# Forming the phases and exponents of lag factors with TensorE instead of VectorE and ScalarE, in an S4 convolution and SwiGLU kernel

## The chip, the cores and the metric

The kernel runs on one core of a Trainium2 chip. The core has five engines, each with a queue of its own that is worked off in order: TensorE (PE, matmuls and transposes; its weight loads are shown as PEld), VectorE (DVE), ScalarE (ACT), GpSimd (POOL) and SyncE (SP, which issues most DMAs). Matmul results land in PSUM, everything else lies in SBUF or in DRAM. The metric is the time of one execution in microseconds on the device; less is better.

## The reference

Two layers of two blocks each, on a sequence of L = 2048 rows of D = 512 channels. The first block is a state space convolution (N = 128 states for each channel), the second a SwiGLU feed-forward net. Cut to what matters:

```python
dt = exp(log_dt)[:, None]                       # one for each channel
logdA = dt * (A_re + 1j * A_im)                 # [D, N]
dB = dt * (B_re + 1j * B_im)
P = exp(logdA[:, :, None] * arange(L))          # [D, N, L]
K = einsum("dn,dnl,dn->dl", Cc, P, dB).real     # the filter, one for each channel
y = irfft(rfft(pad(u)) * rfft(pad(K)))[:L] + u * Dskip

x = x + A_ref(layernorm(x))                     # convolution with K
x = x + (silu(n @ w_gate) * (n @ w_up)) @ w_down    # n = layernorm(x)
# both twice, with the same weights and the same K
```

The change touches only the way in which the factors of P are made. A power l of the exponential is split as l = 32 a + b. For each channel d and state n the kernel needs the phase th = dt * A_im / (2 pi) and the rate rho = dt * A_re. The *lag factors* are, for a = 1 to 64, exp(32 a rho) times cosine and sine of the turns 32 a th; the *small powers* are exp(b (rho + 2 pi i th)) for b = 1, 2, 4, 8, 16, out of which all b below 32 are multiplied together. TensorE then sums over n the product of the two, which gives K at all lags.

## The kernel before

The states n lie on the 128 partitions. The filters are made in stage 1, a loop over eight chunks of DC = 64 channels; behind it come the convolutions by DFT and the feed-forward blocks for eight blocks of 512 rows. In stage 1 the order of ACT, DVE and PE is written out by hand (a `manual_schedule`): generators (`gen_turns`, `gen_reduce`, `gen_trig`, `gen_exp`, `gen_g`, `gen_e`) issue one step each time that `take` asks for it, and each engine works its steps off in the order of issue. POOL and SP run their own issues in order as well. The loop body of iteration i does several things side by side: the lag sums of chunk i, the products of chunk i+1, the phases, sines and exponents of chunk i+2. The first two chunks are made in a head in front of the loop, and the lag sums of the last chunk behind it.

For one chunk, by function and line of the kernel before:

- `gen_turns`: DVE forms the turns 32 a th for a = 17 to 32 in `t16` (L349, 1024 elements for each partition), and the turns of the five small powers in `xi` (L352, 320 elements). The factors stand in `am`, a table of 21 columns.
- `gen_reduce`: ACT rounds to whole turns by writing an integer (L360 for the small powers, L366 for six pieces of `re`, since a = 1 to 16 are halves, quarters and so on of the upper ones); DVE subtracts (L369, and L372 six times). What is left is below half a turn.
- `gen_trig`: ACT takes Abs (L379), sine (L380) and cosine (L381), in three trios: the small powers, the upper half of a, the lower half.
- `gen_exp`: ACT takes exponentials of rho with 32 a as its scale, five for the small powers (`mz`, L389), 20 for `re` (a to 32) and 19 for `mu` (a = 33 to 63) at L394, and fills the other a by squares (L397).
- `gen_e`: DVE multiplies exponentials into cosines and sines (L407, L410, L413, L416).
- `gen_g`: DVE multiplies `mz` into the small powers (L424), starts with the weights w0 (L427 to L431), and doubles the powers in the levels 1, 2, 4, 8, 16 (L437, L441, L445, L446).
- `lags` (L456, L457): PE sums over the states, 128 matmuls into `pk`, in a large PSUM buffer. `spread_in` (ACT, `ks`, L462), `spread` (PE, `kp`, L472) and a copy on ACT (`kt`, L949) bring the filter into the form that the spectra need.
- `spectra`: PE multiplies by the DFT matrix (`pw`, L493, eight matmuls for each of four spectra), ACT copies out (`s1`, L502), POOL combines (L504), SP stores.

Between these steps stand pieces of other work: `second` and `direct` (spectra of the input blocks, `pf`, L276, copied out by ACT, L279), and `norms` (ACT squares, L306, and PE sums `nrm`, L310, for the scale factors of the weights). There are two large PSUM buffers (`pbig`: pk, kp and others) and four small ones (`psml`: pw, pf, nrm and others), each handed out in turn, so that a matmul into a buffer waits for the engine that reads the one before it there.

In the head, `turns()` scales rho and th and takes exponents and turns between the statistics of the first x rows.

## Time and profile before

| what | value |
| --- | --- |
| median of 3 runs | 1213.28 us (1213.07 to 1215.39) |
| profiled execution, span from first to last instruction | 1210.1 us; no other time is shown for it |
| PE busy in the span | 1104.0 us (91%) |
| DVE | 1048.5 us (87%) |
| ACT | 646.3 us (53%) |
| POOL | 187.8 us (16%) |
| DMA moved | 138.66 MB |

The first row is what is compared. The others belong to one profiled execution, whose span is 3.2 us below the median. Busy shares are means over the whole span: the first quarter, the stage that the change touches, looks different from the rest. In the page's row of 40 slices (30 us each), DVE stands at 8 to 9 tenths and ACT at 7 to 9 in the first nine slices, PE at 7 to 9 behind the first; from the tenth slice on PE is at 8 to 9 tenths in all but the last few and ACT falls to 2 to 7.

In rows of the trace, "out<-in" are the program's names of the tiles, "128x1024 f32" is partitions by elements, xN the number of instructions in a group, then come busy time in us, and the mean of one in ns. A row of the timeline has start and length in us, engine, line, operation, and, in brackets, how long the engine had stood idle before and what released it. "clock" is the TensorE clock that the chip granted, as a share of the full one.

### The profile page before, as it was taken

The numbers are of one execution on the slowest core, as the hardware profiler recorded it, in microseconds if no ns is written. First come the engines' busy times: TensorE is split into PE (matmuls) and PEld (weight loads), VectorE is DVE, ScalarE is ACT, GpSimd is POOL, SyncE is SP. The second block draws the span as 40 slices with busy tenths as digits, with TensorE's granted clock in tenths as the row PEclk, the third lists the DMA queues.
The fourth block names the chain that finished last, engine by engine and source line by source line (L and its number), as shares of the span: only waits on it lengthen the run. The fifth ranks groups of instructions, "written<-read, shape, count | busy, mean of one in ns | idle before, by whom it ended". The sixth has DMA issues, their size and how long they took to land.

```text
span 1210.1 us, 25368 instructions
## 1 busy us (share of the span) xinstructions
PE 1104.0 (91%) x10220; PEld 858.5 (71%) x10220; DVE 1048.5 (87%) x1677; ACT 646.3 (53%) x1392; POOL 187.8 (16%) x209
## 2 busy tenths in 40 slices
PE   3877988888978998989999999999999999999998
PEld 2755766666976776868686777778686776867875
DVE  8999999999869999999998999999992799983221
ACT  7999999973265545526753524664431553324111
POOL 1116343453220010101100000121000010000000
PEclk9999998889999999999999999999999999999999
DMA  6223233236389427433245353424433144311000
GB/s 226 96 88 92 72 89 86 73 107 184 116 285 264 127 67 199 133 118 88 62 157 140 105 179 133 125 79 146 140 118 129 33 119 132 117 58 44 14 23 18
DMA packets 134857, 138.66 MB, mean 115 GB/s; under 512 B 75921, under 2 KB 85137, under 8 KB 134738
## 3 DMA queue, kind: packets, MB, share of 16 engines
q1 hardware_dynamic: 132178, 128.64, 35.4%
q0 software_dynamic: 2560, 8.39, 2.0%
q8 instruction: 80, 1.31, 0.5%
q14 instruction: 39, 0.32, 0.1%
HBM read 98.71 MB, written 28.31 MB: 105 GB/s over the span
## 4 chain that ended last, share of the span: by engine, by line
DVE 32%; PE 27%; issue 5%; DMA 4%; ACT 2%; POOL 2%; SPq 1%; DVEq 0%; ACTq 0%; POOLq 0%
DVE t L683 5%; PE pgu L807 5%; PE pgu L808 5%; PE pgu L809 5%; DVE yk L686 4%; DVE z L216 3%; DVE yk L683 3%; PE py L821 3%; PE py L822 3%; PE py L823 3%; PE pi L702 2%; DVE sg L813 2%; DVE hl L815 1%; DVE yl L216 1%; DVE bt L216 1%
## 5 line engine op out<-in xcount | busy, mean ns | idle before, releaser
L807 PE MATMUL pgu<-mix,wsl 128*128 128x256 f16 x1280 | 350.5, 274 | 7.9 <-DVE sg L813 4.4
L809 PE MATMUL pgu<-mix,wsl 128*128 128x256 f16 x1280 | 350.5, 274 | 1.2 <-DVE wsl L579 1.2
L808 PE MATMUL pgu<-mix,wsl 128*128 128x256 f16 x1280 | 350.4, 274 | 0.0
L808 PEld LDWEIGHTS <-wsl 128*128 128x128 f16 x1280 | 125.8, 98 | 24.6 <-issue 8.6
L821 PE MATMUL py<-wsl,hh 128*128 128x512 f16 (+1 forms) x352 | 134.6, 382 | 9.3 <-DVE xg L826 5.3
L809 PEld LDWEIGHTS <-wsl 128*128 128x128 f16 x1280 | 125.8, 98 | 16.5 <-DVE wsl L579 1.5
L807 PEld LDWEIGHTS <-wsl 128*128 128x128 f16 x1280 | 125.8, 98 | 15.8
L823 PE MATMUL py<-wsl,hl 128*128 128x512 f16 (+1 forms) x352 | 134.4, 382 | 2.4 <-DVE hl L815 2.4
L812 ACT ACTIVATE sg<-pgu,sc 128x512 f32<-128x512 f32 x80 | 54.5, 682 | 128.8 <-PE pgu L809 110.9
L822 PE MATMUL py<-wsl,hh 128*128 128x512 f16 x320 | 122.1, 382 | 0.0
L683 DVE TENSOR_TENSOR t<-uu,w 128x1024 f32<-128x1024 f32 x96 | 116.8, 1217 | 5.5 <-DMA uu<-udr 5.3
L686 DVE TENSOR_TENSOR yk<-yk,t 128x1024 f32<-128x1024 f32 x96 | 116.7, 1215 | 0.1
L493 PE MATMUL pw<-kt,ek 128*128 128x256 f32 (+2 forms) x420 | 105.4, 392 | 0.0
L813 DVE SCALAR_TENSOR_TENSOR sg<-pgu,sc,sg 128x512 f32<-128x512 f32 x80 | 59.6, 744 | 52.3 <-ACT sg L812 52.0
L702 PE MATMUL pi<-yl,mix 128*128 128x256 f16 x672 | 91.4, 273 | 5.5 <-ACT yl L691 3.5
L493 PEld LDWEIGHTS pw<-kt,ek 128*128 128x128 f32 x420 | 83.9, 208 | 11.9
L814 ACT ACTIVATE hh<-sg 128x512 f16<-128x512 f32 x80 | 50.0, 626 | 67.6 <-DVE sg L813 67.6
L211 POOL TENSOR_TENSOR rs<-mv,mhalf 128x2 f32<-128x2 f32 (+1 forms) x21 | 38.7, 1845 | 275.7 <-ACT mv L210 275.6
L260 PE MATMUL pf<-z,eh 128*128 128x256 f16 x576 | 74.4, 272 | 1.6 <-ACT z L250 1.6
L702 PEld LDWEIGHTS <-mix 128*128 128x128 f16 x672 | 65.3, 98 | 14.3 <-issue 3.9
L691 ACT ACTIVATE yl<-mix,sy 128x512 f16<-128x512 f32 x56 | 40.2, 717 | 61.4 <-DVE mix L688 61.2
L504 POOL COPY w0r<-s 128x128 f32<-128x128 f32 x29 | 48.1, 1659 | 141.7 <-ACT s L502 122.2
(221 smaller groups left out, 2292.0 us busy)
## 6 DMA issues: line engine op xcount, KB each, us to landing
w<-wdr SPq DMA_DIRECT2D x96, 256.0 KB, 2.8
uu<-udr SPq DMA_DIRECT2D x96, 256.0 KB, 3.0
udr<-u POOLq DMA_DIRECT2D x32, 256.0 KB, 2.8
wdr<-wo SPq DMA_DIRECT2D x96, 64.0 KB, 2.0
udr<-u SPq DMA_DIRECT2D x16, 256.0 KB, 2.5
n<-ndr SPq DMA_DIRECT2D x16, 256.0 KB, 3.0
n<-xdr SPq DMA_DIRECT2D x4, 1024.0 KB, 6.0
xg<-in_A_u_dram SPq DMA_DIRECT2D x3, 1024.0 KB, 7.4
```

The costliest lines, as they stand in the source:

```text
L260: PE.matmul(pf[:, o], lhsT=e, rhs=m, start=k == 0, stop=k == len(terms) - 1)
L493: PE.matmul(pw[:, i], lhsT=e, rhs=kt[:, :, c + 4 * k0:4 * k1:4, :].rearrange("p g k d -> p k g d"), start=c == 0, stop=c == 3)
L683: V.tensor_tensor(t, uu.unsqueeze(1).to_broadcast([P, 2, 2, HD]), w.unsqueeze(2).to_broadcast([P, 2, 2, HD]), OP.mult)
L686: V.tensor_tensor(yk, yk, t, OP.add)
L702: PE.matmul(pi[:, o], lhsT=e, rhs=m, start=k == 0, stop=k == len(terms) - 1)
L807: PE.matmul(o, lhsT=wgu(wi, k, 0)[:, fs], rhs=nh[:, k], start=k == 0, stop=False)
L808: PE.matmul(o, lhsT=wgu(wi, k, 0)[:, fs], rhs=nlo[:, k], start=False, stop=False)
L809: PE.matmul(o, lhsT=wgu(wi, k, 1)[:, fs], rhs=nh[:, k], start=False, stop=k == 3)
L813: V.scalar_tensor_tensor(sg, pgu[:, 1], sc6[:, 4:5], sg, OP.mult, OP.mult)
L821: PE.matmul(py[:, r], lhsT=hh[:n, f, rc], rhs=wd(f, 0)[:n], start=f == 0, stop=False)
L822: PE.matmul(py[:, r], lhsT=hh[:n, f, rc], rhs=wd(f, 1)[:n], start=False, stop=False)
L823: PE.matmul(py[:, r], lhsT=hl[:n, f, rc], rhs=wd(f, 0)[:n], start=False, stop=f == FT - 1)
```

## The change

PE now multiplies rates by a table. The table `am` becomes 1712 columns wide: for 16 channels at a time, it has the factors 32 a for a = 1 to 63 (exponents, `TA`), 32 a for a = 1 to 32 (phases, `TM`) and 1, 2, 3, 4, 8, 16 (small powers, `TZ`), each in the row of its own channel and nought in those of the others, and this three times, once for each bf16 part of the rate. It is loaded as float32 (128 x 1712, 0.88 MB), fourth on SP's queue, ahead of x and B, into `amf`, and ACT converts it to bf16 in `tabs` (L893).

- `gen_parts` (new, for two chunks at a time): ACT takes the bf16 part of rho and th (L365), DVE the residue (L367), ACT its bf16 part (L369), DVE the rest (L371), and SP issues two DMA transposes (L373) that put rows of (rho or th, part, channel) on the partitions. It runs for chunks 0 and 1, and 2 and 3, in the head, and for the pairs behind them in the iterations 1 and 3.
- `args` (new, L377): one bf16 matmul with 112 rows for a group of 16 channels.
- `gen_turns`: four such matmuls of 512 columns into two large PSUM buffers `pp`, and four of 96 into a small one, `pz`.
- `gen_reduce`: ACT rounds from PSUM (L404, twice 1024 and once 384), DVE subtracts (L407, the same three).
- `gen_trig`: the same trios (L414 to L416), channels 0 to 31 first, then 32 to 63, small powers last.
- `gen_exp`: four matmuls of 96 and one exponential for `mz` (L425), then eight times one matmul into a small buffer `pm` (L377) and one exponential out of it (L435), four for `re`, four for `mu`. The squares are gone.
- `gen_g`: six small powers instead of five; the powers 1, 2, 3 are made in one step (L474, L475, L477, L478), then levels 4, 8, 16 as before.
- Loop and head ask for the steps in another order. In the body, two of the four `mu` exponents of chunk i+1 and the fourth spectrum of chunk i-1 stand between the lag sums and `ks`, and the last two operations of `gen_g` stand behind the last of `gen_e`.

The core of the diff:

```diff
+    am = np.zeros((2, 4, 16, NA), np.float64)
+    ta, tm, tz = am[..., :1008], am[..., 1008:1520], am[..., 1520:]
+    zs = (1, 2, 3, 4, 8, 16)
+    for d in range(16):
+        ta[0, :3, d, 63 * d:63 * d + 63] = 32.0 * np.arange(1, 64)
+        tm[1, :3, d, 32 * d:32 * d + 32] = 32.0 * np.arange(1, 33)
+        for x in range(2):
+            tz[x, :3, d, (16 * x + d) * NZ:(16 * x + d + 1) * NZ] = zs
...
+    def gen_parts(ch):
+        src = rt[:, :, ch * DC:(ch + 2) * DC].rearrange("p x (g d) -> p x g d", d=16)
+        hi, mid, lo = (pt[:, :, :, :, q].rearrange("p c g x d -> p x (c g) d") for q in range(3))
+        A.activation(hi, src, AF.Copy)
+        yield
+        V.tensor_tensor(r1, src, hi, OP.subtract)
+        yield
+        A.activation(mid, r1, AF.Copy)
+        yield
+        V.tensor_tensor(lo, r1, mid, OP.subtract)
+        for c in range(2):
+            nc.sync.dma_start_transpose(lts[(ch + c) % 3], pt[:, c].rearrange("p g x q d -> p (g x q d)"))
+        yield
+    def args(o, ch, g, tab):
+        PE.matmul(o, lhsT=lts[ch % 3][:112, g], rhs=tab, start=True, stop=True)
...
     def gen_turns
-        V.tensor_tensor(t16, am[:, 5:].unsqueeze(1).to_broadcast([P, DC, 16]),
-                        t_.unsqueeze(2).to_broadcast([P, DC, 16]), OP.mult)
-        V.tensor_tensor(xz[1], am[:, :5].unsqueeze(2).to_broadcast([P, 5, DC]), t_.unsqueeze(1).to_broadcast([P, 5, DC]), OP.mult)
+        for h in range(2):
+            pp = pbig([P, 32, 32], "pp")
+            for g in range(2):
+                args(pp[:, 16 * g:16 * g + 16], ch, 2 * h + g, TM)
...
     def gen_reduce
-            A.activation(k, src, AF.Copy, scale=1.0 / st)
-            V.scalar_tensor_tensor(*part, OP.mult, OP.subtract)
+        for p, k in zip(pz, ks):
+            A.activation(k, p, AF.Copy)
+        for p, k, o in zip(pz, ks, outs):
+            V.tensor_tensor(o, p, k, OP.subtract)
...
     def gen_exp
-                A.activation(o[:, :, a - a0], r_, AF.Exp, scale=32.0 * a)
+                pm = psml([P, 16, 32], "pm")[:, :, :n]
+                args(pm, ch, g, TA[:, :, a0:a0 + n])
+                A.activation(ts[2][:, 16 * g:16 * g + 16, 1:] if a0 else re[:, 16 * g:16 * g + 16, 1:33], pm, AF.Exp)
...
     def gen_g
-        for n in (1, 2, 4, 8, 16):
+        zr, zi = (t[:, :3].rearrange("p l d -> p d l").unsqueeze(1).to_broadcast([P, 2, DC, 3]) for t in xz)
+        new, tmp = g[:, :, :, 1:4], tmp8[:, :, :, :3]
+        V.tensor_tensor(new, g[:, :, :, 0:1].to_broadcast([P, 2, DC, 3]), zr, OP.mult)
+        V.tensor_tensor(tmp, g[:, ::-1, :, 0:1].to_broadcast([P, 2, DC, 3]), zi, OP.mult)
+        V.tensor_tensor(new[:, 0], new[:, 0], tmp[:, 0], OP.subtract)
+        V.tensor_tensor(new[:, 1], new[:, 1], tmp[:, 1], OP.add)
+        for lv, n in ((3, 4), (4, 8), (5, 16)):
...
     for i in range(NCH - 1):
-            take(ex, 100)
+            take(ex, 3)
             take(sp, 2)
+            take(ex, 3)
             norm_units(3, 9)
             norm_units(0, 0)
+            take(ex, 3)
```

How the order of the queues moves is shown at three places. First, PE behind the lag sums `pk` of a chunk in the middle of the loop. Before, the fourth spectrum `pw` and then the sums `nrm` follow at once:

```order
L457 MATMUL pk<-im,g 32x64
L493 MATMUL pw<-kt_489,ef 128x256
L493 MATMUL pw<-kt_489,ek_84 128x256 x3
L493 MATMUL pw<-kt_489,ef 128x256
L493 MATMUL pw<-kt_489,ek_84 128x256 x3
L310 LDWEIGHTS onesb
L310 MATMUL nrm<-sq,onesb 128x344
```

In the changed kernel PE at the same place has matmuls of rates (in the transposed parts `tt`) by the table (`tabs`) into `pm`, ahead of that spectrum and behind it:

```order
L503 MATMUL pk<-im,g 32x64
L377 LDWEIGHTS tt
L377 MATMUL pm<-tabs,tt 128x16x31
L539 MATMUL pw<-kt_465,ef 128x256
L539 MATMUL pw<-kt_465,ek_85 128x256 x3
L539 MATMUL pw<-kt_465,ef 128x256
L539 MATMUL pw<-kt_465,ek_85 128x256 x3
L377 LDWEIGHTS tt
L377 MATMUL pm<-tabs,tt 128x16x31
```

The spectrum and all behind it, `nrm` and the spreading `kp` among it, have moved behind exponent matmuls. Second, PE between the first and the second spectrum of the same iteration's own chunk. Before, one follows the other:

```order
L493 MATMUL pw<-kt_489,ef 128x256
L493 MATMUL pw<-kt_489,ek_83 128x256 x3
L493 MATMUL pw<-kt_489,ef 128x256
L493 MATMUL pw<-kt_489,ek_83 128x256 x3
L493 MATMUL pw<-kt_489,ef 128x256
L493 MATMUL pw<-kt_489,ek_84 128x256 x3
```

Now PE has two exponent matmuls between them (`wx` is another place of transposed parts):

```order
L539 MATMUL pw<-kt_465,ef 128x256
L539 MATMUL pw<-kt_465,ek_84 128x256 x3
L539 MATMUL pw<-kt_465,ef 128x256
L539 MATMUL pw<-kt_465,ek_84 128x256 x3
L377 LDWEIGHTS wx
L377 MATMUL pm<-tabs,wx 128x512
L377 LDWEIGHTS wx
L377 MATMUL pm<-tabs,wx 128x512
L539 MATMUL pw<-kt_465,ef 128x256
L539 MATMUL pw<-kt_465,ek_85 128x256 x3
```

The two matmuls use the small PSUM buffers that spectra and exponents share. Third, ACT behind the copy `ks` in an odd iteration. Before, ACT rounds the turns that lie in SBUF (`xi`, `t`), in seven pieces:

```order
L462 ACTIVATE ks<-pk 128x1024
L360 ACTIVATE xr<-xi 128x320
L366 ACTIVATE re<-t_996 128x64x16
L366 ACTIVATE re<-t_996 128x64x8
L366 ACTIVATE re<-t_996 128x64x4
L366 ACTIVATE re<-t_996 128x64x2
L366 ACTIVATE re<-t_996 128x64 x2
L502 ACTIVATE s_1093<-pw 128x512
L379 ACTIVATE xr<-xi 128x320
```

Now ACT rounds three pieces out of PSUM, and in iterations 1 and 3 the two steps of `gen_parts` (`btl<-rt` is L365's bf16 part) stand behind them:

```order
L508 ACTIVATE ks<-pk 128x1024
L404 ACTIVATE re<-pp 128x32x32 x2
L404 ACTIVATE xr<-pz 128x384
L365 ACTIVATE btl<-rt 128x2x8x16
L369 ACTIVATE btl<-btl 128x2x8x16
L548 ACTIVATE s_1032<-pw 128x512
L414 ACTIVATE re<-im 128x32x32
```

The rounding of the large pieces has moved ahead of that of the small powers, and the spectrum's copy stands behind the parts.

More of the change, by code (lines that the diff above doesn't have):

```diff
@@ L882 @@
         take(fw[3], 1)
+        for f in fw[4:6]:
+            next(f)
         for h in range(2):
@@ L936 @@
             take(sp, 1)
+            take(rd, 1)
             kp = spread(i, ks)
@@ L947 @@
                 take(tr, 1)
+            else:
+                tr = iter(())
             kt = kt2[:, i % 2]
```

240 lines of the change are left out of this document (130 added, 110 removed).

## The prediction

> **What bounds the kernel now.** I read the page's first line, the span, then the busy time by stretches, cut at two marks of VectorE's own timeline: 57.93 us, where it begins the products of chunk 1 (L424), and 288.17, where it begins the first L683 after the last chunk.
>
> ```profile
> span 1210.1 us, 25368 instructions
> ```
> ```profile
> 57.93:259.00 201.07, 167.72 (x2227) 129.14 (x2220) 200.53 (x275) 188.29 (x488) 85.12 (x77) 0.91 0.29 82
> 259.00:288.17 29.17, 24.87 (x441) 19.52 (x444) 28.89 (x38) 13.15 (x39) 15.91 (x13) 1.00 0.44 127
> ```
>
> The columns are length, busy PE, PE loads, DVE, ACT, POOL, granted clock, DMA share, GB/s. In the loop over chunks DVE works 200.53 of 201.07 us: it is the bound. ACT works 188.29 and PE 167.72 at a mean clock of 0.91, so both have less than a fifth to spare. The change touches only this first stage; all behind it starts when the last chunk is done, so what this stage gains or loses passes through whole.
>
> **What DVE sheds.** Groups of the first 300 us, eight chunks; the first four rows are by line, the others keep shapes apart.
>
> ```profile
> L349 DVE TENSOR_TENSOR t<-am,th 128x1024 f32<-128x1024 f32 x8 | 10.9, 1368 | 0.0
> L352 DVE TENSOR_TENSOR xi<-am,th 128x320 f32<-128x320 f32 x8 | 4.7, 585 | 0.0
> L369 DVE TENSOR_TENSOR xi<-xi,xr 128x320 f32<-128x320 f32 x8 | 4.4, 546 | 0.1
> L372 DVE SCALAR_TENSOR_TENSOR im<-t,re 128x64 f32<-128x64 f32 (+4 forms) x48 | 27.1, 597 | 0.0
> ```
> ```profile
> L372 DVE SCALAR_TENSOR_TENSOR im<-t,re 128x1024 f32<-128x1024 f32 x8 | 9.7, 1213 | 0.0
> L437 DVE TENSOR_TENSOR g<-g,xr 128x512 f32<-128x512 f32 x8 | 6.3, 783 | 0.0
> L437 DVE TENSOR_TENSOR g<-g,xr 128x256 f32<-128x256 f32 x8 | 3.3, 418 | 0.0
> L437 DVE TENSOR_TENSOR g<-g,xr 128x128 f32<-128x128 f32 x8 | 3.3, 408 | 0.0
> L445 DVE TENSOR_TENSOR g<-g,tmp 128x128 f32<-128x128 f32 x8 | 2.3, 284 | 0.0
> L445 DVE TENSOR_TENSOR g<-g,tmp 128x64 f32<-128x64 f32 x8 | 3.4, 425 | 0.0
> ```
>
> Phases: (10.9 + 4.7 + 4.4 + 27.1) / 8 = 5.9 us a chunk go. Levels 1 and 2 go, each shape twice (L441 and L446 repeat them): 2 x (0.408 + 0.418 + 0.284 + 0.425) = 3.1. In come two subtractions of 1024 from PSUM, 2 x 1.21 by the 1024 row, one of 384 at about 0.6, the joint step (two of 384, two of 192: 2 x 0.6 + 2 x 0.37, between the neighbouring rows), and half of two 256-element operations for the parts, 0.4: 5.4. So DVE sheds 3.6 a chunk, some 21 us over the six full iterations. If PSUM made the three subtractions half as dear again, 1.5 of that would go. This is the gain on offer, and it counts only as long as DVE waits for nobody.
>
> **Who waits now.** Steps that one engine did from its own inputs become chains: PE multiplies, ACT rounds or exponentiates, DVE subtracts, ACT takes sines. In each iteration the order has ACT and PE alternate, each behind the other in its queue. So I walk one iteration by rows. First ACT, then PE (times are starts; the difference of two starts is what the first costs):
>
> ```profile
> 169.11 0.47 ACT L379 ACTIVATE xr<-xi 128x320 f32<-128x320 f32 x1 [0.65 <-DVE xi L369]
> 169.60 1.28 ACT L380 ACT_TABLE_LOAD   x1
> 170.90 0.47 ACT L380 ACTIVATE xi<-xi 128x320 f32<-128x320 f32 x1
> ...
> 171.72 1.00 ACT L949 ACTIVATE kt<-kp 128x1024 f32<-128x1024 f32 x1
> 172.63 1.09 ACT L379 ACTIVATE re<-im 128x1024 f32<-128x1024 f32 x1
> ...
> 175.85 0.58 ACT L279 ACTIVATE u<-pf 128x512 f32<-128x512 f32 x1
> ...
> 184.44 1.23 ACT L306 ACTIVATE sq<-st 128x344 bf16<-128x344 f32 x3
> ...
> 186.16 0.58 ACT L502 ACTIVATE s<-pw 128x512 f32<-128x512 f32 x1
> 186.65 1.91 ACT L394 ACTIVATE re<-rho 128x64 f32<-128x64 f32 x12
> ```
> ```profile
> 191.93 0.34 PE L456 MATMUL pk<-re,g 128*32 128x64 f32 x8
> ...
> 197.34 0.70 PE L493 MATMUL pw<-kt,ef 128*128 128x256 f32 x2
> ...
> 200.90 0.60 PE L310 MATMUL nrm<-sq,onesb 128*128 128x344 bf16 x3
> 201.43 0.64 PE L472 MATMUL kp<-ks,ident 128*32 128x256 f32 x8
> ...
> 204.35 0.70 PE L276 MATMUL pf<-n,ef 128*128 128x256 f32 x2
> ...
> 207.91 0.59 PE L493 MATMUL pw<-kt,ef 128*128 128x256 f32 x2
> ```
> ```profile
> 64.94 1.42 PE L310 MATMUL nrm<-sq,onesb 128*128 128x512 bf16 x3 [2.03 <-ACT sq L306]
> ...
> 83.79 1.44 PE L310 MATMUL nrm<-sq,onesb 128*128 128x512 bf16 x3 [3.02 <-ACT sq L306]
> ...
> 88.45 0.61 PE L493 MATMUL pw<-kt,ef 128*128 128x256 f32 x2
> ```
> ```profile
> 99.30 0.81 PE L310 MATMUL nrm<-sq,onesb 128*128 128x512 bf16 x3
> ```
>
> ACT: table 1.3, the trio Abs, Sin, Sin of 1024 3.2, that of the small powers 1.3, a copy of 1024 0.9, of 512 out of PSUM 0.5, three squares 1.2. PE: pk 5.4, a spectrum pw 3.5, kp 2.9, pf 3.5, three nrm 0.5, a bf16 matmul of 512 columns 0.25 (0.81 for three).
>
> Rows have the lines of the kernel before; from here on, lines named without a row are those of the changed kernel. Time 0 is the start of pk. The matmul of the second mu exponent now stands behind pk: 5.7. The fourth spectrum follows to 9.2, and only behind it the third mu matmul, 9.4. ACT: that exponent to 9.9, squares 11.1, the last mu 11.6, ks 12.5, the first rounding of phases 13.4. DVE's order has L464 to L470 (some 2.3), four products of 1024 (4.8), the joint step (1.9) and level 4 (two of 512, two of 256: 2.4) ahead of L407, which needs this rounding: ready at 11.4, it waits for 13.4 and is through at 14.6. ACT meanwhile: second rounding 14.3, small one 14.8, s1 15.3, then table and first trio 19.8, kt 20.7, second trio 23.9, u 24.4, small trio 25.7, table 27.0, mz 27.5, first exponent 28.0. PE: kp waits for L407 (their big PSUM buffer), 14.6 to 17.5, pf 21.0, pz 21.3, first spectrum 24.8, pm 25.0. The next pm needs the small PSUM buffer that mz empties, 27.5, and the second spectrum the buffer of the first exponent: it starts at 28.0 instead of 25. To 31.5; nrm and pm 32.3; third spectrum 35.8; two pm, and the next pk starts at 36.3. DVE, from 14.6 on, has 17 us left and ends near 32: it is idle for 4 and no longer sets the pace. PE does 29.7 us of work and waits for the rest; the three bf16 us that it got are on the path.
>
> Iteration 0 has no fourth spectrum: 33.9. Iterations 1 and 3 also form parts: ACT's L365 stands behind the roundings, 15.2, DVE's L367 needs it and stands ahead of L407. Behind L367 come two operations of 512, one of 1024, two of 256 and the low part before L407 (0.42 + 2 x 0.78 + 1.21 + 2 x 0.42 + 0.42 = 4.4): L407 ends near 20.9 instead of 14.6, ACT's sines start 5.6 later, so 41.9. Six iterations: 33.9 + 2 x 41.9 + 3 x 36.3 = 226.6. Before, between the first pk and that of iteration 6:
>
> ```profile
> L456 PE MATMUL pk<-re,g x1024: 217/219/314, 57.1 to 294.3; 128*32 128x64 f32 x171
> ```
> ```profile
> 260.29 0.34 PE L456 MATMUL pk<-re,g 128*32 128x64 f32 x8
> ```
>
> 260.3 - 57.1 = 203.2. So +23.4 at full clock. The clock: behind a pause of 3.02 us three nrm took 1.44 instead of 0.81 and full speed was back at 88.45, 4.7 us later, which costs half of that, 2.3; behind 2.03 us it was slow as well (1.42). The walk has a pause of 2.5 in every iteration and one of 6 in iterations 1 and 3: eight, at 0 to 2.3 each. I take 0.8, since the short ones are at the lower end of what the rows show: 6.4. Loop: +29.8, from +23 to +42. Should PE's waits overlap better than in the walk, +8 is left, or nothing.
>
> The Trainium skill (TensorE: Matmul & The Clock Gate, section Part 1: The HAM clock gate) says that the clock falls back only after about a whole idle window of 3.4 us. By it only the two long pauses would be charged and the forecast would be some 3 us lower; the row with a pause of 2.03 speaks against so high a threshold, since its matmuls were slow already.
>
> **The head.** Rows of the first chunk: DVE, the queue of SP, landings.
>
> ```profile
> 24.45 0.49 DVE L424 TENSOR_TENSOR xr<-xr,mz 128x320 f32<-128x320 f32 x1
> ...
> 30.95 1.21 DVE L407 TENSOR_TENSOR im<-im,re 128x1024 f32<-128x1024 f32 x1
> ```
> ```profile
> 11.53 3.17 SPq L304 DMA_DIRECT2D st<-in_B_w_down_dram  x3
> ```
> ```profile
> 0.00:25.00 25.00, 4.20 (x12) 3.37 (x13) 19.27 (x48) 16.01 (x33) 4.29 (x21) 1.00 0.75 274
> ```
> ```profile
> mix<-nn SPq DMA_TRANSPOSE x60, 2.4
> ```
>
> The table now has 0.88 MB ahead of x and B: at 274 GB/s and 0.75 busy, 2.4 us more. The two transposes stand behind the three st loads, whose issue ended at 14.7: 17.1, and landing takes 2.4 in a quiet queue, more in this full one; I take 22 (19.5 to 24.5). Two matmuls 22.5, rounding 23.4, L407 24.7, table and trio 29.2, trio 32.4, small trio 33.7, table 35.0, mz 35.5: L464 there, where the same product (L424) was at 24.45. DVE has nothing else in its order: +11. Its next work up to L447 took 6.5 (24.45 to 30.95), less the removed L349 and L352, 1.5: 40.5; but ACT's fourth exponent waits for two PE steps behind mz (a pf of 3.5, cold up to 7): 42. Then 3.8 to chunk 1's L407 at 45.8, which needs roundings behind four mu exponents and pf: 47.9. From its end, 49.1, DVE has 9.3 us, to 58.4, and there L367 waits for L365, which stands on ACT behind both trios, four scalings of x1, the small trio and three u: 63.7. Another 11.4 to the last product of chunk 0 (L492): pk starts at 75.1, against 57.1: +18 (+13 to +21).
>
> **The tail.** In iteration 6 nothing is made for later chunks. L447 runs at 0.5 behind pk, and the rest of the chunk is 24.5: DVE is free at 25, against 288.17 - 260.29 = 27.9: -3.
>
> Sum: +18 + 29.8 - 3 = +45. It is made against the profiled execution, of which the page gives the span, 1210.1; the median of the runs, 1213.28, lies 3.2 above it, and the sum goes on top of that: 1258. Its own range is 1231 (head +13, loop +8) to 1273 (head +21, loop +42).
>
> **Rivals.** (1) DVE keeps the pace and the waits are covered in the loop, while the head still costs: 203.2 - 21 there, +18, -3: 1207, faster. For it speaks that DVE is busy in 200.5 of 201.1; it needs the first rounding by 11.4, and pk alone ends at 5.4 with 3.5 of spectrum, 1.2 of squares and four short ACT steps behind. 0.12. (2) The head is covered too: 1213 - 21 - 7 (two chunks) - 3 = 1182. Against it: L464 cannot start before mz. 0.04. (3) PE goes cold in every pause at the full 2.3, and takes pf of the head at half rate: 1258 + 12 + 3 = 1273. For it: 0.91 is the mean clock already. 0.15. (4) Losses and gains cancel within 0.2% (2.4 us, about what a measurement of this kernel can tell from no change): 0.03. The walked case has the rest, 0.66. [...]
>
> So slower by over 0.2%: 0.79 (the walked and the cold case, less 0.02 for the edge); within: 0.04; faster: 0.17. The range: 1223 takes in a loop as long as before with a head of +13, less 3; 1276 the cold case with 3 more of the head's bound. Outside are (1), (2), (4) and a rest of the walked case, 2 in 10 together.
>
> **What will show it.** Right, if L464 of chunk 0 starts near 35 and pk near 75, if in iterations 2, 4 and 5 the second spectrum waits for ACT's first exponent and the chunks are 36 to 38 us apart, those of iterations 1 and 3 over 40 with DVE waiting for L365, and if DVE's busy share in the loop falls below 0.9. Wrong, if DVE has no waits there: then chunks come every 30 us and the time is near 1207.

## The result, and the profile after

The changed kernel takes 1266.43 us (median of 4, 1265.23 to 1268.5), the kernel before 1213.17 beside it: ratio 1.0437, 95% interval 1.0403 to 1.0471, 53 us more. The profiled execution's span is 1263.4. Cut at the first lag sums of the head (L456 before, L502 after), those of iteration 6 and VectorE's first L683 (now L729), the busy times by stretches of the changed kernel are (columns as before):

```profile
0.00:80.62 80.62, 41.16 (x173) 31.35 (x174) 47.65 (x86) 43.91 (x61) 7.78 (x26) 0.95 0.44 138
80.62:314.17 233.55, 191.03 (x2398) 135.57 (x2398) 183.25 (x226) 151.46 (x228) 52.52 (x78) 0.89 0.28 75
314.17:339.41 25.24, 20.32 (x357) 15.31 (x357) 24.51 (x27) 10.94 (x22) 10.98 (x6) 1.00 0.41 124
339.41:1263.40 923.99, 882.67 (x7457) 684.71 (x7455) 766.84 (x1269) 397.89 (x749) 77.29 (x100) 0.99 0.40 118
```

The same cuts in the kernel before:

```profile
0.00:57.05 57.05, 32.17 (x136) 27.47 (x137) 50.99 (x99) 47.89 (x117) 7.66 (x25) 1.00 0.46 166
57.05:260.29 203.24, 169.89 (x2276) 130.81 (x2276) 202.70 (x277) 190.46 (x503) 86.31 (x78) 0.91 0.30 83
260.29:288.17 27.88, 23.58 (x436) 18.73 (x439) 27.60 (x36) 11.86 (x30) 14.72 (x11) 1.00 0.44 129
288.17:1210.10 921.93, 878.37 (x7389) 681.45 (x7377) 767.17 (x1269) 396.11 (x746) 79.14 (x96) 0.99 0.39 118
```

| stretch | before | after | difference | predicted |
| --- | --- | --- | --- | --- |
| head | 57.1 | 80.6 | +23.6 | +18 |
| six iterations | 203.2 | 233.6 | +30.3 | +29.8 |
| end of the stage | 27.9 | 25.2 | -2.6 | -3 |
| all behind it | 921.9 | 924.0 | +2.1 | 0 |

Of the 53 us, 51 lie in stage 1; the 2.1 behind it, where the change has no instruction, stay unexplained. In the loop VectorE was busy 202.7 of 203.2 us and is now busy 183.3 of 233.6: it sheds 19.4 and waits for 50. Its waits in the loop (total, times, longest):

```profile
DVE btl L367 <- ACT btl L365: 18.0, 2, 9.8
DVE im L407 <- ACT re L404: 13.0, 4, 5.0
DVE im L447 <- ACT re L435: 11.6, 5, 5.2
DVE cmx L333 <- PE nrm L330: 6.0, 3, 3.0
```

The last three are waits for what another engine makes out of a third one's work: the rounded phases, the last exponents, the sums of squares. In the first, ACT's part needs no other engine's result, but stands in ACT's queue behind roundings that do. The six iterations by themselves:

```profile
80.62:118.76 38.14, 33.45 (x387) 22.37 (x388) 31.69 (x43) 23.77 (x34) 3.95 (x8) 0.78 0.28 78
118.76:162.15 43.39, 32.18 (x404) 22.39 (x403) 30.93 (x38) 26.61 (x41) 8.27 (x14) 0.88 0.28 71
162.15:198.62 36.47, 31.20 (x403) 22.95 (x402) 29.67 (x35) 24.96 (x39) 10.48 (x14) 0.95 0.27 72
198.62:240.41 41.79, 31.86 (x403) 22.49 (x402) 31.45 (x38) 26.05 (x41) 8.84 (x14) 0.84 0.27 71
240.41:276.37 35.96, 29.50 (x404) 22.12 (x403) 30.19 (x36) 24.98 (x39) 10.74 (x14) 1.00 0.27 74
276.37:314.17 37.80, 32.84 (x404) 23.25 (x403) 29.33 (x36) 25.09 (x39) 10.24 (x14) 0.91 0.32 86
```

Iterations 1 and 3, which form parts, take 43.4 and 41.8; the even ones 36 to 38. No engine fills them: ACT, which had 190 of 203 us, has 151 of 234. Iteration 2 on ACT's timeline shows what it stands for:

```profile
163.58 0.58 ACT L435 ACTIVATE mu<-pm 128x496 f32<-128x496 f32 x1
168.09 0.59 ACT L435 ACTIVATE mu<-pm 128x496 f32<-128x496 f32 x1 [3.94 <-PE pm L377]
...
171.77 0.58 ACT L435 ACTIVATE mu<-pm 128x496 f32<-128x496 f32 x1 [2.61 <-PE pm L377]
...
173.86 1.02 ACT L508 ACTIVATE ks<-pk 128x1024 f32<-128x1024 f32 x1
174.76 1.97 ACT L404 ACTIVATE re<-pp 128x1024 int32<-128x1024 f32 x2
```

The lag sums had begun at 162.15. The second mu exponent comes 5.9 us behind that, because its matmul stands behind the lag sums on PE, the third 9.6, because its matmul stands behind the fourth spectrum, and ks 11.7. Behind ks come the roundings, for which VectorE waits 5.0 us at L407 in this iteration.

### The profile page after: what moved, and what is told of

Its sections match the earlier page's. It is cut to its first block, busy times and chain, and to the rows that moved or that the text cites. A ratio compares the mean times of both kernels' runs of the same rounds, so it can differ in the third digit from the quotient of the medians.

```text
span 1263.4 us, 25289 instructions
## 1 busy us (share of the span) xinstructions
PE 1135.2 (90%) x10380; PEld 866.9 (69%) x10380; DVE 1022.2 (81%) x1605; ACT 604.2 (48%) x1057; POOL 148.6 (12%) x210
## 3 DMA queue, kind: packets, MB, share of 16 engines
q1 hardware_dynamic: 136530, 130.56, 35.5%
## 4 chain that ended last, share of the span: by engine, by line
PE 36%; DVE 19%; DMA 5%; issue 4%; ACT 3%; POOL 2%; SPq 1%; DVEq 0%; POOLq 0%; ACTq 0%
PE pgu L853 6%; PE pgu L854 6%; PE pgu L855 6%; PE py L867 4%; PE py L868 4%; PE py L869 4%; PE pi L748 3%; PE pf L280 3%; DVE t L729 3%; DMA mix<-nn 2%; DVE yk L732 2%; DVE yk L729 2%; DVE z L236 2%; POOL rs L231 1%; DVE bt L236 1%
## 5 line engine op out<-in xcount | busy, mean ns | idle before, releaser
L853 PEld LDWEIGHTS <-wsl 128*128 128x128 f16 x1280 | 125.5, 98 | 15.7
L729 DVE TENSOR_TENSOR t<-uu,w 128x1024 f32<-128x1024 f32 x96 | 117.7, 1226 | 4.5 <-DMA uu<-udr 4.3
L539 PE MATMUL pw<-kt,ek 128*128 128x256 f32 (+2 forms) x420 | 96.6, 368 | 0.0
L539 PEld LDWEIGHTS pw<-kt,ek 128*128 128x128 f32 x420 | 77.2, 192 | 9.0
L280 PE MATMUL pf<-z,eh 128*128 128x256 f16 x576 | 74.8, 273 | 1.6 <-ACT z L270 1.6
L729 DVE TENSOR_TENSOR yk<-u,w0r 128x1024 f32<-128x1024 f32 x56 | 68.5, 1224 | 0.3 <-ACT u L282 0.3
L868 PEld LDWEIGHTS <-hh 128*128 128x128 f16 (+1 forms) x352 | 34.9, 99 | 48.2 <-issue 13.5
L861 DVE TENSOR_TENSOR hl<-sg,hh 128x512 f16<-128x512 f32 x80 | 55.5, 693 | 13.5 <-ACT hh L860 13.4
```

The source lines that it names most:

```text
L280: PE.matmul(pf[:, o], lhsT=e, rhs=m, start=k == 0, stop=k == len(terms) - 1)
L539: PE.matmul(pw[:, i], lhsT=e, rhs=kt[:, :, c + 4 * k0:4 * k1:4, :].rearrange("p g k d -> p k g d"), start=c == 0, stop=c == 3)
L729: V.tensor_tensor(t, uu.unsqueeze(1).to_broadcast([P, 2, 2, HD]), w.unsqueeze(2).to_broadcast([P, 2, 2, HD]), OP.mult)
L853: PE.matmul(o, lhsT=wgu(wi, k, 0)[:, fs], rhs=nh[:, k], start=k == 0, stop=False)
L868: PE.matmul(py[:, r], lhsT=hh[:n, f, rc], rhs=wd(f, 1)[:n], start=False, stop=False)
```

## The experiments

Each run has its ratio to the kernel before, measured beside it on the same chip. "Loop" is the profiled time of the six iterations, "first lag sums" the end of the head.

| run | median | ratio (95% interval) | loop | first lag sums |
| --- | --- | --- | --- | --- |
| changed kernel | 1266.4 | 1.0437 (1.0403 to 1.0471) | 233.6 | 80.6 |
| e1_parts | 1258.9 | 1.0371 (1.0330 to 1.0412) | 225.3 | 80.3 |
| e2_mz | 1276.4 | 1.0519 (1.0466 to 1.0571) | 246.2 | 78.0 |
| e5_round | 1269.2 | 1.0460 (1.0417 to 1.0503) | 232.1 | 78.7 |
| e6_head | 1265.0 | 1.0443 (1.0395 to 1.0492) | 236.9 | 78.9 |
| g1_order | 1280.2 | 1.0536 (1.0494 to 1.0577) | 248.5 | 76.4 |
| e9_warm | 1254.3 | 1.0332 (1.0293 to 1.0372) | 224.4 | 78.4 |
| e8_phases | 1244.5 | 1.0246 (1.0206 to 1.0287) | 211.5 | 77.8 |
| e10_phases_parts | 1227.6 | 1.0093 (1.0060 to 1.0126) | 200.6 | 78.3 |
| e11_act_queue | 1226.7 | 1.0094 (1.0061 to 1.0126) | 200.6 | 78.0 |
| e13_x1_late | 1229.1 | 1.0112 (1.0069 to 1.0155) | 202.4 | 74.8 |
| e12_levels | 1268.3 | 1.0430 (1.0382 to 1.0478) | 235.4 | 78.4 |
| e4_joint | 1206.2 | 0.9929 (0.9901 to 0.9956) | 203.4 | 57.1 |

The head's end differs by up to 4 us between kernels whose head has the same steps (76.4 to 80.6), so a difference of that size between two of them says nothing by itself; what it comes from is seen below, at the head. My theory is that of the prediction: chains from engine to engine set the length of an iteration. The rival is that TensorE does, by its 160 matmuls more and by its clock.

**The parts (e1_parts).** The first step, ACT's L365, is issued at the start of the iteration, VectorE's L367 behind L407; the third and fourth steps follow behind kt and the second trio.

```diff
+            take(parts, 1)
             take(ex, 3)
...
-            for g in (gg, ge, gg, ge, parts, gg, ge, parts, gg, ge, parts, gg, parts):
+            for g in (gg, ge, gg, ge, gg, ge, gg, ge, gg):
...
             take(rd, 2)
+            take(parts, 1)
```

> Iterations 1 and 3 issue ACT's bf16 part (L365) ahead of everything else of the iteration and VectorE's residue (L367) behind the subtractions of the phases (L407). The waiting theory: in the changed kernel VectorE stood 9.8 and 8.2 us in front of L367 in these two iterations, against 1.7 to 5.0 in front of L407 in the even ones; they come down from 43.4 and 41.8 us to 37 or 38, so 1266 becomes about 1256 (1252 to 1260). The rival, that TensorE's 160 more matmuls and its colder clock set the pace: no change, 1264 to 1269.

Measured: 1258.9, and iterations 1 and 3 by the busy times in stretches:

```profile
117.71:155.54 37.83, 33.19 (x403) 23.23 (x402) 30.58 (x38) 26.49 (x41) 11.18 (x14) 0.91 0.29 79
...
194.77:232.27 37.50, 34.14 (x404) 24.08 (x403) 30.47 (x38) 25.91 (x41) 11.72 (x14) 0.86 0.30 79
```

From 43.4 and 41.8 to 37.8 and 37.5, while iteration 2 between them went from 36.5 to 39.2: 8.2 less in the loop, and the time as expected by the waiting theory. The wait in front of L367 was on the path, but not with its whole size: 18.0 us of waiting went, the two iterations came 9.9 shorter, and VectorE now waits 20.4 us at L407 in the loop instead of 13.0.

**The matmuls that wait for mz (e2_mz).**

```diff
-                take(ex, 1)
-                take(sp, 1)
-                take(ex, 4)
+                take(sp, 3)
+                take(ex, 3)
+                take(sp, 1)
+                take(ex, 2)
+                take(sp, 1)
                 norm_units(3, 9)
-                take(sp, 2)
```

> In the loop the small exponents' matmuls (pz) and the first exponent matmuls stand behind the second spectrum, and two exponents are read before the third. The walk of the prediction had TensorE stand 2.5 us in front of an exponent matmul and 0.5 in front of the second spectrum in every iteration: by it about 1250 (six times 2.7 less). By the rows of the changed kernel these waits are only some 4 us in all (2.1 and 2.0 for mz, 0.3 for the exponent), so that by them about 1262 (1258 to 1266). The rival (TensorE's work and clock): no change.

Measured: 1276.4, slower by 10 where both theories had no change or a gain. In the changed kernel TensorE had stood for mz for 4.1 us in the whole loop, so there was little to take away, and what took its place was longer: a copy of the first spectrum is now ahead of mz on ACT, VectorE waits for mz in front of L464 in four iterations (0.9 to 2.1), and three times over 5 us for sums of squares, whose matmuls stand behind the third spectrum now (5.0, 5.6, 5.7 us). L367's wait grew from 18.0 to 20.4 us.

**The roundings ahead of the mu exponents (e5_round).**

```diff
-            take(ex, 3)
-            take(sp, 2)
-            take(ex, 3)
-            norm_units(3, 9)
-            norm_units(0, 0)
-            take(ex, 3)
-            take(gg, 2)
+            take(ex, 1)
             if more:
                 next(tn)
             ks = spread_in(pk)
+            take(sp, 2)
             if more:
                 take(tn, 2)
                 rd = gen_reduce(ts[i + 2], pz)
                 take(rd, 3)
+            take(ex, 5)
+            norm_units(3, 9)
+            norm_units(0, 0)
+            take(ex, 3)
+            take(gg, 2)
```

> In the loop ks and the three roundings (L404) stand ahead of the last three mu exponents on ACT, and the phase matmuls directly behind the lag sums on TensorE. The waiting theory: ks starts 6 us behind the lag sums instead of 11.7, the roundings come before VectorE is at L407, and its waits of 1.7, 5.0, 1.4 and 4.9 us there and half of the 9.8 and 8.2 in front of L367 go, as does TensorE's wait for L407 in front of kp (20.6 us in six): 13 to 22 less, 1244 to 1253. The rival (TensorE's work and clock): no change, 1264 to 1269.

Measured: 1269.2, no gain, which is what the rival expected. But the waits that were to go did go: in the loop VectorE never stands at L407. In their place PE waits for ACT, and VectorE for the last exponents; one row of PE's waits (from the first lag sums to those of the last chunk) and one of VectorE's timeline:

```profile
PE pm L377 <- ACT mu L435: 11.8, 11, 1.6
```
```profile
193.39 1.23 DVE L447 TENSOR_TENSOR im<-im,re 128x1024 f32<-128x1024 f32 x1 [6.75 <-ACT re L435]
```

In iteration 2 the matmuls of the mu exponents, now in a row, each wait for ACT to empty a small buffer, and kp begins 14.0 us behind the lag sums instead of 15.0. At its end VectorE comes 6.75 us too early to L447, since the last exponents' matmuls still stand behind the third spectrum on PE. So L407 was not where the iteration is decided; my expectation took a wait away and counted it as time.

**Several moves together (g1_order).** On e1_parts: phases directly behind the lag sums, the second input spectrum ahead of kp, kt behind the first trio, the second spectrum ahead of the small exponents.

```diff
             take(ex, 2)
+            if more:
+                f = second(*sec[i])
+                next(f)
+            take(ex, 2)
+            take(sp, 1)
...
             kp = spread(i, ks)
-            if more:
-                f = second(*sec[i])
-                next(f)
```

> The kernel with the parts moved, with another order in the loop: the first phases stand directly behind the lag sums, the second input spectrum fills the time until L407, kt is behind the first trio and a copy, the second spectrum stands ahead of the small exponents, and two exponent matmuls ahead of the third spectrum. The waiting theory, walked by rows at full clock: the next lag sums 31.5 to 33 us behind the last instead of 36, six times: about 1238 (1230 to 1245). If TensorE's work at the clock that it gets is the bound (33 to 34 us busy in an iteration at 0.8 to 0.9): not under 1245.

Measured: 1280.2, the slowest of all. VectorE's waits over the whole stage:

```profile
DVE cmx L333 <- PE nrm L330: 30.6, 4, 13.2
DVE im L407 <- ACT re L404: 21.6, 6, 5.2
```

The maximum over the sums of squares (L333) is VectorE's next operation where it stands in the order, and my order had put the squares and their matmuls later: VectorE stood there up to 13.2 us. An order of three queues that is right for one chain is wrong for another. By the number alone this is what was written down for the rival (not under 1245); as these new waits explain it, it decides nothing between the two.

**The clock (e9_warm).** On e1_parts, TensorE repeats phase matmuls (same data to the same place) where it would wait.

```diff
+            if more:
+                next(tn)
+                for _ in range(3):
+                    args(pz[0][:, :16], i + 2, 0, TM)
             norm_units(0, 0)
...
+                for _ in range(4):
+                    for g in range(4):
+                        args(keep[0][:, g], i + 2, g, TZ[:, 1])
```

> The kernel with the parts moved (1259), with idle matmuls: TensorE repeats phase matmuls (same data, same place) where it would wait for the squares, for ks and for L407, 1.3, 1.3 and 1.3 us in each iteration, so that it is not idle there. If the clock is what costs (the six iterations of that kernel took 35.7 at a clock of 1.00, and 37.4 to 39.2 at 0.80 to 0.91; walked at full clock they would be 33.9 for the first and 36 for the rest, 11 us in all), the clock in the loop goes to 0.95 or more and the time falls by 5 to 11, to 1248 to 1254. If the waits are what costs and the clock only follows: 1257 to 1262, as the repeats lie in the waits.

Measured: 1254.3 against 1258.9, between the two ranges expected (1248 to 1254, 1257 to 1262), and the intervals of the ratios overlap. The first four iterations:

```profile
78.39:114.43 36.04, 31.36 (x410) 22.93 (x410) 33.08 (x43) 23.41 (x34) 4.97 (x8) 0.92 0.28 81
114.43:152.32 37.89, 32.13 (x425) 23.36 (x425) 30.59 (x38) 26.26 (x41) 10.68 (x14) 1.00 0.31 81
152.32:189.02 36.70, 31.40 (x425) 23.32 (x425) 29.69 (x35) 24.98 (x39) 10.29 (x14) 1.00 0.27 73
189.02:227.28 38.26, 33.06 (x425) 24.50 (x424) 30.85 (x38) 25.57 (x41) 11.11 (x14) 0.96 0.29 77
```

And the whole loop, of e1_parts and of this run:

```profile
80.33:305.66 225.33, 196.75 (x2398) 139.83 (x2398) 181.27 (x226) 151.57 (x228) 57.09 (x78) 0.89 0.29 78
```
```profile
78.39:302.80 224.41, 194.19 (x2529) 143.16 (x2529) 183.73 (x226) 150.13 (x228) 58.42 (x78) 0.96 0.28 77
```

The clock goes from 0.89 to 0.96, and the loop from 225.3 to 224.4. That is the net of the clock and of the repeats themselves, and it is uneven: iterations 0 and 2, where the clock rose from 0.80 to 0.92 and from 0.87 to 1.00, came 1.3 and 2.5 us shorter, the other four together 3.0 longer. So the run does not give the price of the clock alone. A hint at it is in the changed kernel, whose iterations 2, 4 and 5 run nearly the same instructions: they took 36.5, 36.0 and 37.8 us at a clock of 0.95, 1.00 and 0.91, with TensorE busy for 31.2, 29.5 and 32.8. There slower matmuls and longer iterations go together, by up to 2 us. Against the clock as the maker of the 30 us lost in the loop speaks e10_phases_parts below, whose loop takes 200.6 at the same 0.89.

**Exponents by ACT again (e8_phases).** Phases stay with TensorE; gen_exp forms 45 exponents of 64 elements and the squares from rho as before, at the same places of ACT's order.

```diff
-                args(pm, ch, g, TA[:, :, a0:a0 + n])
                 yield
-                A.activation(ts[2][:, 16 * g:16 * g + 16, 1:] if a0 else re[:, 16 * g:16 * g + 16, 1:33], pm, AF.Exp)
+                for a in aa[5 * k:5 * k + 5]:
+                    A.activation(o[:, :, a - a0], r_, AF.Exp, scale=32.0 * a)
```

> The changed kernel with exponents formed by ACT from rho with a scale, as before (six for the small powers, 39 for re and mu, and the squares), at the same places of ACT's order; phases are still formed by TensorE. TensorE loses 12 matmuls and 2.2 us a chunk and no longer stands behind mz or an exponent; ACT gets about 5 us a chunk more (39 exponents of 0.16, the squares, less eight of 0.55). The waiting theory: ACT's chain to ks and to the last exponents gets longer by what TensorE gains, 1266 stays within 1258 to 1274. If TensorE's added work is the cost: 15 less, about 1251.

Measured: 1244.5, 22 less. My own bounds (1258 to 1274) did not hold, and by what I had written down this is the rival's side (15 less) and beyond it: I had ACT's added work lengthen a chain that ACT, with 151 of 234 us, had the room for. The loop is 22.1 shorter, and the even iterations come close to VectorE's pace (29.3 us busy of 31.9), as iteration 2 shows:

```profile
151.75:183.65 31.90, 28.18 (x392) 21.96 (x391) 29.28 (x36) 29.75 (x78) 8.88 (x13) 0.95 0.29 81
```

ACT works 29.8 us in it instead of 25.0, and the iteration is 4.6 shorter. In the changed kernel's loop ACT stood 62.7 us for matmuls of exponents, in 19 waits:

```profile
ACT mu L435 <- PE pm L377: 43.4, 12, 11.7
ACT re L435 <- PE pm L377: 19.3, 7, 3.4
```

Here none are left. TensorE's share: it was busy 175.3 us in the loop instead of 191.0, and if all 15.7 lay on the path, at least 6 of the 22 are something else, which fits the round trip ACT, PE, ACT; how the rest divides between trip and work no run shows.

**Both (e10_phases_parts).** The edits of e1_parts and e8_phases together.

> Exponents by ACT from rho, and the parts moved as well. If the two costs are apart: the two odd iterations, 40.2 and 40.1 us with exponents by ACT alone, come down to the 32 to 34 of the even ones, and 1244 becomes 1233 (1229 to 1237); what is left above the kernel before, some 18, would then be the head (its first lag sums at 78 instead of 57), less some 3 of the tail and of the loop. If a wait of another kind takes the place of the parts' (as when roundings were moved): 1240 to 1245.

Measured: 1227.6, just below the 1229 to 1237 expected. Iterations 1 and 3, and the whole loop:

```profile
111.55:145.50 33.95, 29.61 (x391) 22.04 (x390) 28.93 (x34) 31.58 (x81) 9.49 (x14) 0.90 0.33 88
...
178.89:212.87 33.98, 29.59 (x392) 22.55 (x391) 29.96 (x35) 30.98 (x81) 9.42 (x15) 0.90 0.33 87
...
78.28:278.90 200.62, 175.71 (x2324) 133.30 (x2325) 183.16 (x224) 181.74 (x467) 55.55 (x78) 0.89 0.31 85
```

They fall from 40.2 and 40.1 to 34.0, and the loop to 200.6, less than before the change (203.2). With the exponents where they were and the parts out of the way, forming phases by TensorE (and the joint step) costs the loop nothing, though it gains only 2.6 us of the 19.5 that VectorE sheds. The granted clock is 0.89, as in the changed kernel's loop, which takes 33 us more; so the clock does not tell the two apart. What stays is the head: first lag sums at 78.3 instead of 57.1.

**The head (e6_head, e11_act_queue, e13_x1_late).** In the changed kernel the head's chain is, on three engines' timelines:

```profile
16.99 0.39 DVE L371 TENSOR_TENSOR btl<-btl 128x256 bf16<-128x256 f32 x1
...
41.20 0.56 DVE L464 TENSOR_TENSOR xr<-xr,mz 128x384 f32<-128x384 f32 x1 [7.62 <-ACT mz L425]
...
69.95 0.43 DVE L367 TENSOR_TENSOR btl<-rt,btl 128x256 f32<-128x256 f32 x1 [4.88 <-ACT btl L365]
```
```profile
19.56 2.97 SPq L373 DMA_TRANSPOSE tt<-btl  x2
```
```profile
26.78 1.89 PE L377 MATMUL pp<-tabs,tt 112*128 112x512 bf16 x4 [18.94 <-DMA tt<-btl]
```

The first low parts are ready at 17.4, the transposes are issued at 19.6 and land at 26.7. The first run moved the exponents of chunk 0 ahead of the input spectra, and L365 ahead of the scalings of x1:

```diff
         take(ex, 3)
+        take(ex, 7)
...
+        parts = gen_parts(2)
+        take(parts, 1)
         for c in range(4):
             A.activation(x1[:, c], x1[:, c], AF.Identity, scale=stats_x[0][:, c:c + 1], bias=stats_x[1][:, c:c + 1])
```

> Only the head is changed: the exponents of chunk 0 stand ahead of the first input spectra on TensorE, and ACT's bf16 part for chunks 2 and 3 ahead of the scalings of x1. The waiting theory: the fourth exponent, which VectorE waits for until 48.5, is there near 44, and the 4.9 us wait for L365 at 70 goes: pk of chunk 0 starts 6 to 9 us earlier than 80.6, and 1266 becomes 1258 to 1261. If the head is bound by TensorE's eight input spectra (28 us at full clock), 0 to -2.

Measured: 1265.0, which is the second case expected (0 to -2); first lag sums at 78.9, within the spread of the unchanged head. Both waits went, and VectorE then stood 8.06 us at L407 of chunk 1, whose matmuls are behind three input spectra. The first of these stood behind a pause of 9.0 us of TensorE and ran mostly at half speed, 6.3 us instead of 3.5. The second run and the third stand on e10_phases_parts: transposes of the first parts issued by ACT, and x1's load issued later, and by ACT.

```diff
-            nc.sync.dma_start_transpose(lts[(ch + c) % 3], pt[:, c].rearrange("p g x q d -> p (g x q d)"))
+            (nc.scalar if ch == 0 else nc.sync).dma_start_transpose(lts[(ch + c) % 3], pt[:, c].rearrange("p g x q d -> p (g x q d)"))
```

> As the run before, and the two transposes of the first parts are issued by ACT, which is idle then, instead of SP, where three loads of st stand ahead of them. If the queue position is what costs: phases of chunk 0 start 2 us earlier than 26.8, and so do the first lag sums; 1231 against 1233. If the landing is bound by the full transfers around it: both where they were, no change.

```diff
-    nc.sync.dma_start(x1, x[0, T:2 * T, :].rearrange("(c p) d -> p c d", p=P))
...
-        take(rd, 3)
+        take(rd, 1)
+        nc.scalar.dma_start(x1, x[0, T:2 * T, :].rearrange("(c p) d -> p c d", p=P))
+        take(rd, 2)
```

> As the kernel with exponents by ACT and the parts moved (1227.6), and the 1 MB load of x1 is issued behind the first rounding, at 28, instead of ahead of the transposes. If the landing of the transposes (6.7 us from issue, behind some 8 MB of loads at 400 GB/s) sets the start of chunk 0's phases: 2.5 us earlier, at 24 instead of 26.5, and its first lag sums at 76 instead of 78.3, 1225. If the transposes take that long by themselves: phases at 26 to 27, no change.

Issued by ACT, the transposes began at 18.97, only 0.3 earlier, though the parts were ready at 16.8, and the phases at 26.25 instead of 26.55. So that run hardly moved the issue, and its lack of gain (1226.7 against 1227.6) says little of the queue. A run from above says more: g1_order's trace has no st load in the first 40 us, so nothing of st stands ahead of the transposes on SP.

```profile
17.17 3.29 SPq L373 DMA_TRANSPOSE tt<-btl  x2
```

Issued 2.4 us earlier than in the changed kernel, they land just as long behind their issue (6.6 us), and the phases start at 24.3 instead of 26.8. So with the st loads out of the way they start earlier; whether it is the loads' place in the queue or their traffic that held them back, no run tells, and ACT's issue came late all the same. With the load of x1 out of the way, two rows tell (PE's timeline; DMA issues to 31 us, landing from issue in us):

```profile
23.03 1.89 PE L376 MATMUL pp<-tabs,tt 112*128 112x512 bf16 x4 [15.21 <-DMA tt<-btl]
```
```profile
tt<-btl SPq DMA_TRANSPOSE x2, 5.0
```

Phases start 3.5 us earlier (landing in 5.0 instead of 6.7, issue 1.8 earlier), VectorE gets mz 3.5 earlier, and the first lag sums start at 74.75 instead of 78.28. The medians (1229.1 against 1227.6, with overlapping intervals) don't show the 3.5; the profiled loop was 1.8 longer.

The start of the phases also explains the spread of the head's end: in e2_mz, e5_round, g1_order and e9_warm the lag sums come 52.1 to 52.2 us behind it. In the changed kernel and e1_parts they come 53.8 behind it: there the second input spectrum took 5.2 us instead of 3.6, partly at half speed, and VectorE waited 2.1 us instead of 0.4 for the fourth exponent, whose matmul stands behind it.

**The joint step (e4_joint, e12_levels).** Alone in the kernel before, and undone in the changed one:

```diff
-        for n in (1, 2, 4, 8, 16):
+        V.tensor_tensor(new, g[:, :, :, 0:1].to_broadcast([P, 2, DC, 3]), zr, OP.mult)
+        V.tensor_tensor(tmp, g[:, ::-1, :, 0:1].to_broadcast([P, 2, DC, 3]), zi, OP.mult)
...
+        for lv, n in ((3, 4), (4, 8), (5, 16)):
```

> The kernel before with one part of the change alone: the first three powers in one step, with six small powers instead of five; phases and exponents stay where they were. VectorE is the bound there (200.5 of 201 us): per chunk levels 1 and 2 (3.1) go, the joint step (1.9) comes, and 64 elements more in four operations and one exponent more (0.2): 1.0 less, seven or eight times, so 1212 becomes 1204 to 1207. If ACT or TensorE stand close behind VectorE (ACT works 188 of 201), only 0 to 3 are gained.

> The changed kernel with the joint step undone: levels 1 and 2 as before, on the same six small powers. Alone, in the kernel before, the joint step gained 9 us, since VectorE is the bound there. The waiting theory: in the changed kernel VectorE stands for other engines behind these operations (L407 and L367), so it has the 1.1 us a chunk to spare: -1 to +3 against 1266. If VectorE's work still sets the pace: 7 to 9 more, 1273 to 1275.

Measured: alone 1206.2 against 1215.2, ratio 0.9929, the only run that beats the kernel before. Undone in the changed kernel: 1268.3, ratio 1.0430 against 1.0437, no difference. That fits the waiting theory: where VectorE stands for others, its work is free. But the gain of the first is not where I expected it. In its profiled execution the loop is as long as before (203.4), as is the head; 6.0 of the 7.1 us that the spans differ lie behind the last lag sums (from 922.9 to 917.0), where this edit has no instruction. VectorE stays busy throughout the loop, and its other operations took longer there; the same group before and with the joint step:

```profile
L446 DVE TENSOR_TENSOR g<-g,tmp 128x512 f32<-128x512 f32 x18 | 13.1, 726 | 0.0
```
```profile
L456 DVE TENSOR_TENSOR g<-g,tmp 128x512 f32<-128x512 f32 x18 | 14.5, 807 | 0.0
```

GpSimd was busy 112 us in that loop against 86, which may be why; no run tests it. That it is faster is measured; through which stage stays open.

## Why the prediction was right, and where not

1258 was forecast, 1223 to 1276 the range, and 1266.4 came. It lies 8 above the walked case and 7 below the cold one (1273), so the number alone does not choose between these two.

**What VectorE sheds.** 21 us were worked out for six iterations, 19.4 measured. Reading PSUM did not make the subtractions dearer: L407's 1024 elements took 1217 ns, as the 1213 of the row that was used. And the gain counted for nothing, as said, because VectorE waits.

**The walk of an iteration.** 36.3, 33.9 and 41.9 were walked for an even iteration, the first and the odd ones; 36.0 to 37.8, 38.1, and 43.4 and 41.8 were measured. The chain was the one in the rows: second mu exponent 5.7 walked and 5.9 measured in iteration 2, the start of ks 11.6 and 11.7, kp 14.6 and 15.0. VectorE stood at L407 at 8.7 instead of 11.4, since L464 to L470 were done before the lag sums began. Of the signs named, L464 and pk of chunk 0 came late (41.2 and 80.6 for 35 and 75); the chunks' distances, the waits for L365 and VectorE's busy share of 0.78 came as said, and the second spectrum's weights waited for ACT's first exponent in iterations 2 and 5, in 4 for mz. That exponents made by PE are the larger cost of the loop is shown by e8_phases (-22 us; how much of it is the wait and how much PE's work stays open), that the parts' L365 and L367 are by e1_parts (-8 in the loop) and e10_phases_parts (-11 beside e8_phases in the loop).

**What failed inside it.** First, "the next pm needs the small PSUM buffer that mz empties" was walked as 2.5 us in every iteration, 3.0 with the second spectrum's buffer; in the loop TensorE's matmuls waited 4.1 us for mz in all, and its weight loads of the second spectrum 8.7 for mz and the first exponent, half of the 18 walked. e2_mz, which moved these matmuls, was slower. Second, the wait at L407 was walked as if the iteration hung on it; e5_round took it away and gained nothing: in its trace mu exponents and the third spectrum held the last exponents back just as long. Several chains end within a few us of each other, so one of them alone is worth little. Third, the term for the clock: +6.4 was summed, as 0.8 for each of eight pauses. The loop came 6.9 above the walk at full clock, but not in that way: 4.2 of it lie in the first iteration, which was charged one pause and had the coldest clock, 0.78; the two odd ones have 1.4 together, the even ones 1.3. How much of this is the clock stays open, as e9_warm gives only a net of 0.9 with the repeats in it. That 29.8 and 30.3 agree so closely is in part luck.

**The head.** +18 (13 to 21) was forecast and +23.6 measured, outside that range; kernels with this head have 19 to 24. The step that failed is the landing of the transposes: "I take 22", and it was 26.7. They were issued at 19.6 instead of 17.1 and landed 6.7 us later instead of 4.9, with the loads ahead still moving some 400 GB/s until 23. What follows is late by about as much: L464 41.2 against 35.5, lag sums 80.6 against 75.1. On top of e10_phases_parts, x1's load issued later brought the lag sums to 74.75.

**Tail and rivals.** -3 and -2.6. VectorE does not keep the pace (rival 1: it is busy 0.78 of the loop), and the head is not covered (rival 2). The cold clock (rival 3) came true in part. Its loop term, eight pauses at 2.3, is 18.4, and the loop came 6.9 above the walk at full clock; for the head it adds 3, and the half-speed spectrum there cost 1.7.

## What to carry to other kernels

Moving work off the busiest engine did not pay here, as the result had to travel through queues of engines that were occupied with other things: each exponent became a trip from ACT's place to PE's queue and back, and VectorE, less busy by a tenth, waited for it. Before such a move, walk one iteration queue by queue and look for every in-order engine that the new steps cross. And a wait that is taken away is worth only the distance to the next chain; where several end together, the steps have to leave their queues, as exponents formed by ACT itself did, not to change places in them.

## What the runs showed of the hardware

TensorE's speed fell without a long pause. In front of the lag sums of chunk 0 it had stood for 6.6 us, and the clock was down to 0.50; by 84 us it was at 1.00 again. Then it fell once more, as three stretches of two microseconds show (the clock stands third from the end):

```profile
84.00:86.00 2.00, 1.40 (x97) 1.23 (x89) 2.00 (x5) 0.00 (x0) 0.00 (x0) 1.00 0.00 0
88.00:90.00 2.00, 0.50 (x2) 0.19 (x2) 2.00 (x4) 2.00 (x5) 0.00 (x0) 1.00 0.00 0
92.00:94.00 2.00, 1.27 (x6) 0.46 (x5) 0.32 (x2) 1.87 (x3) 0.00 (x0) 0.50 0.43 159
```

The longest wait of TensorE since the lag sums was 1.7 us, and matmuls of the input spectrum were at half speed until 103.8:

```profile
89.36 0.89 PE L330 MATMUL nrm<-sq,onesb 128*128 128x512 bf16 x2 [1.70 <-ACT sq L326]
...
100.18 1.22 PE L296 MATMUL pf<-n,ef 128*128 128x256 f32 x2
101.20 2.77 PE L296 MATMUL pf<-n,ek 128*128 128x256 f32 x6
103.76 0.67 PE L296 MATMUL pf<-n,ef 128*128 128x256 f32 x2
104.26 1.46 PE L296 MATMUL pf<-n,ek 128*128 128x256 f32 x6
```

The first pair took 1.22 and the next 0.67, with waits of 1.7, 0.7 and 0.95 us and the narrow matmuls of kp ahead of it. By the rule of the Trainium skill (TensorE: Matmul & The Clock Gate, section Part 1: The HAM clock gate) that the prediction weighed, the clock falls back after an idle window of about 3.4 us; this fall had no wait over 1.7 us ahead of it since the clock was last full. Filling such waits with repeats went with a clock of 0.92 in this iteration instead of 0.80, and of 1.00 in the next two.

The first two transposes of the parts landed 6.7 us behind their issue, with 8 MB of loads moving in the first 31 us, and in 5.0 with the 1 MB of x1 issued later. The 60 transposes of `nn` in the kernel before have a median of 2.4.
